# First expert group with seven half products, a ring of five x tiles, and shorter latencies in the planner's table

## The chip, the cores and the metric

The kernel runs on one core of one Trainium2 chip. The metric is the device time of one execution in microseconds (us); the smaller, the better. Five engines work side by side: PE (matrix products), DVE (VectorE), ACT (ScalarE), POOL (GpSimd) and SP, which here issues all DMA transfers.

## The reference

One transformer block, all in float32, with S = 2048 tokens and D = 512:

```python
xn = layernorm(x)
# A: sliding-window attention, 32 heads of 16, window of 256 keys
p = softmax(where(mask, q @ k.T / 4, -1e9));  a = (p @ v) @ wo
# B: 8 experts, F = 1376; top 8 of 8, so every expert counts for every token
gates = softmax(xn @ w_gate)
b = sum(gates[:, e] * (silu(xn @ w1[e]) @ w2[e]) for e in range(8))
out = x + a + b
```

## The kernel before

**Numbers.** Each float32 operand of a product is split into a high and a low half in float16. A product is then three matmuls: high by high, high by low, low by high. The helper `mm3` (lines 259 to 261) writes these three. Each matmul has a weight load (LDWEIGHTS) of its own.

**Tiling of the experts.** The hidden columns of the eight experts are cut into 17 groups of 128-column pairs: for each expert one group of two pairs and one of three, and after expert 3 a mixed group of three pairs from the seams between experts. Tokens are in four blocks of 512 (`tb`). A "double" is the work of `first_products` on two (pair, block) units; there are 70 doubles. Where a group has three pairs, the middle double of three takes the third pair for two token blocks at once.

**First products** (xn by w1) use Strassen's scheme in Winograd's form: seven half products in place of eight. The seven token-side operands ("x factors", numbered 0 to 6) of each block are made once, stored to the DRAM tiles `XS`, and read back for each double by `load_x_part`: 728 loads of 256 KB, all from SP (L710), into a ring of `XB` = 8 tiles `xs`. A load may start when the product that read the tile's old content has ended. A double whose two units have the same block takes seven tiles, a middle double fourteen.

**Second products** (h by w2) come in two forms. `second7` also uses seven half products, in steps of 256 columns on two halves of two PSUM banks, with five evictions by DVE per pair of 128-row stripes (`evict`, e1 to e5). `second` is the plain form: per stripe of 128 rows, for each 128-column piece of the pair, one `mm3` of 512 columns, and one eviction of 512 columns per stripe. Before the change the groups of three pairs of one expert (`part`) and those of two pairs (`seven`) take `second7`, but group 0 is left out of `seven`; group 0 and the mixed group take `second`. For `second7` DVE or POOL form four sums of the activations (`sum7`) and ACT with DVE or POOL split seven factors (`factor7`, tiles `hh` and `hl`, `HB` = 18 of each); w2 is split into four sets of "half weights" A to D (`prep2s`, with four sums by POOL) in place of the two pieces of `prep2`. The half weights lie in `W2B` = 16 slots.

**What sets the order.** The program of every engine is laid out by hand. A planner (`Order`) runs while the program is written: it keeps a clock for PE (`order.t`) and one each for ACT, DVE, POOL and SP, adds a fixed cost for each instruction, and appends an instruction when its inputs are ready by these clocks. A result counts as ready at the planned end plus `LATE` of the engine (for PE: plus `DRAIN`) plus `AGO` = 100 ns; a load on SP is booked with 450 ns for its issue, and then 2000 ns and 899 ns for its data, behind the loads booked before it (`landed`). Before PE's next piece `wait` looks whether its inputs are ready; if not, it puts other work first: steps of attention (`attend`) or second products (`drain_one`); only with none left does it let PE's clock run idle. On the chip each engine runs its list in order and waits on semaphores; the planner's times no longer matter then, only the order that came of them.

Of the kernel before, what the change touches and what calls it, by code (L numbers as in the profile page):

```python
# [18 lines left out]
P = 128  # L19
# [28 lines left out]
HB = 18  # L48
XB = 8
W2B = 16  # L50
# [8 lines left out]
DRAIN = 200  # L59
# [18 lines left out]
LATE = {"A": 100, "V": 80, "G": 80}  # L78
# [172 lines left out]
def tile_attn_moe(ctx: ExitStack, tc: tile.TileContext, x, wqkv, wo, _bx, wg, w1, w2, out):  # L251
# [103 lines left out]
    seven = {g for g, (e, pairs) in enumerate(groups) if len(pairs) == 2 and g}  # L355
# [119 lines left out]

    def prep2(g, i, j, r2, slot, act, dve):
        w = w2s[g, i, j]

        def high():
            w["t"] = moe.tile([P, 2, D], F16, tag=f"w2_{slot}", bufs=1, name=f"w2_{g}_{i}_{j}")  # L480
            nc.scalar.activation(out=w["t"][:, 0, :], in_=r2()[:, j, :], func=AF.Copy, scale=power[g][0][:, 1:2])

        def low():
            nc.vector.scalar_tensor_tensor(
                out=w["t"][:, 1, :], in0=r2()[:, j, :], scalar=power[g][0][:, 1:2], in1=w["t"][:, 0, :],
                op0=ALU.mult, op1=ALU.subtract,
            )

        w["done"] = dve(665, low, [act(615, high, [])])

    def prep2s(g, i, r2, slots, act, dve, gps):
# [3 lines left out]
        def part(src, kind, o, n, hilo):  # L495
            w = w2s[g, i, kind]

            def run():
                if "t" not in w:
                    w["t"] = moe.tile([P, 2, D], F16, tag=f"w2_{slots[kind][0]}", bufs=1, name=f"w2_{g}_{i}{kind}")  # L500
                sc = power[g][0][:, 1:2]
                hi, lo = (w["t"][:, p, o : o + n] for p in range(2))
                if hilo == 0:
                    nc.scalar.activation(out=hi, in_=src(), func=AF.Copy, scale=sc)
                else:
                    nc.vector.scalar_tensor_tensor(out=lo, in0=src(), scalar=sc, in1=hi, op0=ALU.mult, op1=ALU.subtract)
# [190 lines left out]
    x_issued = Event(0)  # L697

    def load_x_part(free, slack):
# [8 lines left out]
        def run():  # L708
            t = moe.tile([P, 2, 2, TB // 2], F16, tag="xs", bufs=XB, name=f"xs{m}_{b[0]}_{b[1]}")
# [456 lines left out]
    def weight_tasks():  # L1166
# [3 lines left out]
        slots2 += [((-2,), None)] * (W2B - 4 - len(slots2)) + [((-1,), {"gone": xn_free})] * 4  # L1170
        preps = {g: [] for g in range(NG)}
# [212 lines left out]
    with tc.tile_pool(name="ph0", bufs=1) as p0:  # L1384
# [183 lines left out]
        def layernorm(tb, slack):  # L1568
# [4 lines left out]
                    moe.tile([P, 2, 2, TB // 2], F16, tag="xs", bufs=XB, name=f"x{r}{c}").rearrange(  # L1573
                        "p r k t -> p r (k t)"
                    )
# [378 lines left out]
        for tb in range(4):  # L1954
# [20 lines left out]
            if tb == 3:  # L1975
                for n in range(XB):
                    had = (16 + n - XB) // 4
# [349 lines left out]
```

## Time and profile before

| | us |
|---|---|
| median of 3 runs (2070.85 to 2072.74) | 2072.7 |
| the profiled execution | 2072.15 |
| its span, first to last instruction | 2070.4 |
| PE busy in the span | 2034.6 (98%) |
| DVE busy | 1732.4 (84%) |
| ACT busy | 1356.9 (66%) |
| POOL busy | 997.1 (48%) |

The busy time of an engine is the time in which at least one of its instructions is in work. On PE a matmul of 256 columns is shown with 0.27 us though the next starts 0.11 us later, since they are pipelined; the rate is read from the starts. The idle time of an engine before an instruction is put down to what ended it (the releaser).

### The profile page before, as it was taken

Reading aid. Unit: us, or ns where it says so; the run is one execution under the profiler, and the core shown is the slowest. Engines: PE = TensorE matmul, PEld = TensorE weight load, DVE = VectorE, ACT = ScalarE, POOL = GpSimd, SP = SyncE. Lnnn points to the kernel's source line nnn. Section 1 sums busy time; section 2 is a strip of 40 time slices with the busy share of each in tenths; the row PEclk is TensorE's granted clock in tenths of the full one; section 3 lists DMA queues with packets and bytes.
Section 4 is the critical chain, followed back from the end, with each engine's and each line's share of the span. In section 5 each row is a group of like instructions: output and inputs, shape, how many; then the busy total and the mean of one; then the engine's idle time right before and its main releaser. Section 6 shows DMA issues by size and latency. Waiting matters only on the chain.

```text
span 2070.4 us, 52097 instructions
## 1 busy us (share of the span) xinstructions
PE 2034.6 (98%) x20036; PEld 1687.9 (82%) x20036; DVE 1732.4 (84%) x3594; ACT 1356.9 (66%) x2438; POOL 997.1 (48%) x1113
## 2 busy tenths in 40 slices
PE   7999999999999999999999999999999999999999
PEld 4657788888888888888876688888888888888887
DVE  7547887998889988998866889889988998889967
ACT  5656767666666766775656667676767667766753
POOL 5533545555355544563433445445544455356632
PEclk9999999999999999999999999999999999999999
DMA  6875557455654665476776545664656456645642
GB/s 222 260 239 190 171 186 210 130 156 166 204 148 116 220 203 155 110 214 191 210 214 218 166 137 160 196 171 119 201 178 187 112 177 174 217 126 142 173 151 81
DMA packets 343418, 362.16 MB, mean 175 GB/s; under 512 B 132192, under 2 KB 211040, under 8 KB 343168
## 3 DMA queue, kind: packets, MB, share of 16 engines
q1 hardware_dynamic: 343168, 358.82, 57.8%
q8 instruction: 157, 2.57, 0.5%
q14 instruction: 93, 0.76, 0.1%
HBM read 324.55 MB, written 33.88 MB: 173 GB/s over the span
## 4 chain that ended last, share of the span: by engine, by line
PE 86%; DVE 7%; DMA 3%; ACT 2%; issue 1%; SPq 1%; POOL 0%; DVEq 0%; POOLq 0%; ACTq 0%
PE acc L259 11%; PE acc L260 11%; PE acc L261 11%; PE zx L259 6%; PE zx L261 6%; PE zx L260 6%; PE zy L259 5%; PE zy L261 5%; PE zy L260 5%; PE pv L2142 4%; PE qk L1753 4%; PE st L2110 3%; PE sc L2042 3%; PE vg L1816 2%; DMA r<-in_B_w_dram 2%; DVE x L123 1%
## 5 line engine op out<-in xcount | busy, mean ns | idle before, releaser
L123 DVE SCALAR_TENSOR_TENSOR x<-acc,gsc,x 128x512 f32<-128x512 f32 x616 | 392.2, 640 | 110.9 <-PE acc L261 105.9
L259 PE MATMUL zx<-xs,w 128*128 128x256 f16 x1376 | 375.5, 273 | 2.4 <-DMA xs<-XS 2.3
L261 PE MATMUL zx<-xs,w 128*128 128x256 f16 x1376 | 375.1, 273 | 0.0
L260 PE MATMUL zx<-xs,w 128*128 128x256 f16 x1376 | 375.0, 272 | 0.0
L2096 ACT ACTIVATE pf<-st,esc 128x512 f32<-128x512 f32 (+2 forms) x384 | 245.9, 657 | 105.4 <-PE st L2110 104.1
L259 PE MATMUL zy<-xs,w 128*128 128x256 f16 x1032 | 281.6, 273 | 6.8 <-DMA xs<-XS 3.2
L261 PE MATMUL zy<-xs,w 128*128 128x256 f16 x1032 | 281.3, 273 | 0.0
L260 PE MATMUL zy<-xs,w 128*128 128x256 f16 x1032 | 281.2, 272 | 0.0
L260 PEld LDWEIGHTS <-w 128*128 128x128 f16 x2408 | 235.4, 98 | 49.2 <-issue 11.4
L259 PEld LDWEIGHTS <-w 128*128 128x128 f16 x2408 | 234.9, 98 | 45.1 <-issue 5.2
L123 DVE CUSTOM_DVE_ANT_0 sc<-sc,mask 128x320 f32<-128x320 f32 (+4 forms) x512 | 235.2, 481 | 39.7 <-PE sc L2042 38.2
L261 PEld LDWEIGHTS <-hl 128*128 128x128 f16 x2288 | 222.9, 97 | 44.6 <-POOL hl L123 0.7
L261 PEld LDWEIGHTS <-w 128*128 128x128 f16 x2408 | 234.8, 98 | 28.1
L260 PEld LDWEIGHTS <-hh 128*128 128x128 f16 x2288 | 223.7, 98 | 41.8 <-issue 6.8
L978 ACT ACTIVATE hh<-s 128x512 f16<-128x512 f32 x304 | 186.4, 625 | 107.5 <-DVE s L123 46.7
L259 PEld LDWEIGHTS <-hh 128*128 128x128 f16 x2288 | 223.2, 98 | 37.7 <-issue 5.5
L123 POOL TENSOR_SCALAR_AFFINE_SELECT pf<-pf 128x512 f32<-128x512 f32 (+1 forms) x256 | 155.1, 615 | 184.4 <-ACT pf L2096 94.9
L123 POOL TENSOR_TENSOR hl<-s,hh 128x512 f16<-128x512 f32 x126 | 147.5, 1177 | 85.3 <-ACT hh L978 34.2
L123 POOL TENSOR_TENSOR sums<-r 128x256 f32<-128x256 f32 x162 | 122.8, 758 | 131.7 <-DMA r<-in_B_w_dram 46.8
L123 POOL TENSOR_TENSOR sums<-r,sums 128x256 f32<-128x256 f32 x119 | 90.1, 757 | 157.4 <-DVE hl L123 47.0
L123 POOL TENSOR_TENSOR hl<-zb,hh 128x512 f16<-128x512 f32 x88 | 102.6, 1166 | 118.9 <-ACT hh L978 80.1
L123 DVE TENSOR_TENSOR hl<-s,hh 128x512 f16<-128x512 f32 x178 | 142.1, 806 | 14.1 <-ACT hh L978 13.7
(206 smaller groups left out, 5513.6 us busy)
## 6 DMA issues: line engine op xcount, KB each, us to landing
xs<-XS SPq DMA_DIRECT2D x728, 256.0 KB, 3.2
r<-in_B_w_dram SPq DMA_DIRECT2D x172, 256.0 KB, 3.8
r<-in_B_w_dram SPq DMA_DIRECT2D x80, 512.0 KB, 4.8
OS<-os SPq DMA_DIRECT2D x64, 128.0 KB, 2.1
q<-QS SPq DMA_DIRECT2D x192, 32.0 KB, 2.3
VS<-vt SPq DMA_DIRECT2D x16, 256.0 KB, 2.9
ot<-OS SPq DMA_DIRECT2D x128, 32.0 KB, 2.0
lt<-RS SPq DMA_DIRECT2D x128, 32.0 KB, 2.7
```

What stands on the lines that cost most here:

```text
L123: one = getattr(self.engine, name)(*args, **kw)
L259: nc.tensor.matmul(ps, lhsT=lh, rhs=rh, start=first, stop=False, **kw)
L260: nc.tensor.matmul(ps, lhsT=lh, rhs=rl, start=False, stop=False, **kw)
L261: nc.tensor.matmul(ps, lhsT=ll, rhs=rh, start=False, stop=last, **kw)
L978: nc.scalar.activation(out=h["hi"], in_=src(), func=AF.Copy)
L1753: nc.tensor.matmul(ps, lhsT=a[w][c // 2][:, k, cs], rhs=b[k // 2][:, k % 2, :], start=n == 0 and k == 0, stop=n == 2 and k == KC - 1,)
L1816: nc.tensor.matmul(ps[:, : VW // 2], lhsT=a[k // 2][:, k % 2, ts], rhs=b[2][:, k, ws], start=n == 0 and k == 0, stop=n == 2 and k == KC - 1,)
L2042: nc.tensor.matmul(ps[:, :n], lhsT=s.q[:KR, j * P : (j + 1) * P], rhs=s.k[:KR, cs : cs + n], start=True, stop=True)
L2096: nc.scalar.activation(out=w["pf"][:, j0 * P :], in_=ps[:, j0 * P :], func=AF.Exp, scale=esc)
L2110: nc.tensor.matmul(ps[:, j * P : (j + 1) * P].rearrange("p (b c) -> p b c", c=64), lhsT=s.k[:QR, kc : kc + P], rhs=of_head(s.q[:QR, qc : q ...
L2142: nc.tensor.matmul(ps[VC * j : VC * j + VC, a * P : (a + 1) * P], lhsT=s.v[:, kb, a * VC : a * VC + VC], rhs=w["pf"][:, j * P : (j + 1) * ...
```

## The change

- `seven` takes group 0 too: its second products go through `second7`, its activations through `silu7`, `sum7` and `factor7`, its w2 through `prep2s`.
- The ring of x tiles has `XR` = 5 tiles (tags xs0 to xs4) in place of 8. The three other tiles of the old ring, xs5 to xs7, become slots for half weights (`place2`) once the last products of phase 0 have read them. `W2B` falls to 15, so there are 18 slots. In phase 0 the layernorm still uses all eight.
- `HB` rises from 18 to 19.
- The planner's latencies: `DRAIN` 200 to 110, `LATE` for ACT 100 to 10, for DVE 80 to 40, for POOL 80 to 10.

```diff
-HB = 18
+HB = 19
 XB = 8
-W2B = 16
+XR = 5
+W2B = 15
...
-DRAIN = 200
+DRAIN = 110
...
-LATE = {"A": 100, "V": 80, "G": 80}
+LATE = {"A": 10, "V": 40, "G": 10}
...
-    seven = {g for g, (e, pairs) in enumerate(groups) if len(pairs) == 2 and g}
+    seven = {g for g, (e, pairs) in enumerate(groups) if len(pairs) == 2}
...
+    def place2(slot, name):
+
+        if slot < W2B:
+            return moe.tile([P, 2, D], F16, tag=f"w2_{slot}", bufs=1, name=name)
+        t = moe.tile([P, 2, 2, TB // 2], F16, tag=f"xs{XR + slot - W2B}", bufs=1, name=name)
+        return t.rearrange("p r k t -> p r (k t)")
...
-            t = moe.tile([P, 2, 2, TB // 2], F16, tag="xs", bufs=XB, name=f"xs{m}_{b[0]}_{b[1]}")
+            t = moe.tile([P, 2, 2, TB // 2], F16, tag=f"xs{next(x_turn) % XR}", bufs=1, name=f"xs{m}_{b[0]}_{b[1]}")
...
+        slots2 += [((-1,), {"gone": qk_gone[1, 1]})] * (XB - XR)
...
-                for n in range(XB):
-                    had = (16 + n - XB) // 4
+                for n in range(XR):
+                    had = (XB + n) // 4
```

By the two orders the change takes 192 matmuls of 512 columns from PE and adds 336 of 256 columns, and 144 weight loads. DVE gets 16 evictions of 256 columns and 8 of 512 more; ACT 16 instructions more; POOL 50 more, since the planner now gives it more of the sums and low halves; SP has as many DMAs as before, 1994.

On PE, the first second products of group 0, ahead of the change (names: `acc` the PSUM tile, `w2_0_0_0` the first piece of the first pair's weights, `hh` and `hl` the high and low half of the activations, `zy` and `xs` a first product):

```order
L259 LDWEIGHTS hh_2256
L259 MATMUL acc_2310<-w2_0_0_0_1612,hh_2256 128x512
L260 LDWEIGHTS hh_2256
L260 MATMUL acc_2310<-w2_0_0_0_1612,hh_2256 128x512
L261 LDWEIGHTS hl_2257
L261 MATMUL acc_2310<-w2_0_0_0_1612,hl_2257 128x512
L259 LDWEIGHTS w1_0_0_1595
L259 MATMUL zy_2318<-xs3_0_1_2198,w1_0_0_1595 128x256
```

And in the same place with the change (`w2_0_0D` is half weight set D):

```order
L260 LDWEIGHTS hh_2104
L260 MATMUL acc_2273<-w2_0_0D_1612,hh_2104 128x256
L261 LDWEIGHTS hh_2104
L261 MATMUL acc_2273<-w2_0_0D_1612,hh_2104 128x256
L262 LDWEIGHTS hl_2105
L262 MATMUL acc_2273<-w2_0_0D_1612,hl_2105 128x256
L260 LDWEIGHTS hh_2104
L260 MATMUL acc_2273<-w2_0_0D_1612,hh_2104 128x256
```

One `mm3` of 512 columns has become two of 256, one for each pair, and the first of them stands within the first product of the next double; ahead of the change it stood behind that double's third product.

On SP, the start of the first middle double (group 1, third pair, blocks 0 and 1; `xs4_1_0` is x factor 4 for group 1, block 0; `r1` raw weights; `OS` a store of attention), ahead of the change:

```order
L710 DMA xs0_1_0_3191<-XS0_63 128x1024
L710 DMA xs0_1_1_3247<-XS1_64 128x1024
L2160 DMA OS_60<-os_3263 128x256
L710 DMA xs1_1_0_3299<-XS0_63 128x1024
L710 DMA xs1_1_1_3327<-XS1_64 128x1024
L370 DMA r1_2_1_3333<-in_B_w1_dram 128x4x256
L710 DMA xs4_1_0_3381<-XS0_63 128x1024
L710 DMA xs4_1_1_3408<-XS1_64 128x1024
```

With the change:

```order
L719 DMA xs0_1_0_3462<-XS0_63 128x1024
L719 DMA xs0_1_1_3491<-XS1_64 128x1024
L719 DMA xs1_1_0_3544<-XS0_63 128x1024
L719 DMA xs1_1_1_3580<-XS1_64 128x1024
L719 DMA xs4_1_0_3605<-XS0_63 128x1024
L719 DMA xs4_1_1_3640<-XS1_64 128x1024
L719 DMA xs3_1_0_3646<-XS0_63 128x1024
L387 DMA r2_1_1_3659<-in_B_w2_dram 128x512 x2
```

The first seven loads of this double now follow each other with nothing between, and each waits for the tile of the load five ahead of it, not eight.

On DVE, around the first eviction of group 0, ahead of the change (`x0` takes the sum, `ISA sc` is the maximum of attention's scores):

```order
L123 SCALAR_TENSOR_TENSOR t_2437<-t_2428,za_2303 128x512
L123 SCALAR_TENSOR_TENSOR x0_124<-acc_2310,gsc_1871,x0_124 128x512
L123 TENSOR_REDUCE m_2451<-mp_1514 128x2
L123 ISA sc_2461,mt_2309<-sc_2461,mask_106 128x64
L123 ISA mt_2309 128x1
L123 SCALAR_TENSOR_TENSOR x0_124<-acc_2433,gsc_1871,x0_124 128x512
```

With the change (`s7` a sum of activations):

```order
L124 SCALAR_TENSOR_TENSOR x0_124<-acc_2273,gsc_1877,x0_124 128x256
L124 SCALAR_TENSOR_TENSOR zb_2154<-t_2281,zb_2154 128x2x256
L124 TENSOR_TENSOR s7_2318<-za_2064,zb_2154 128x512
L124 TENSOR_TENSOR s7_2331<-s7_2318,za_2064 128x512
L124 TENSOR_TENSOR hl_2329<-s7_2318,hh_2328 128x512
L124 SCALAR_TENSOR_TENSOR za_2348<-zy_2292,s1_2299 128x2x256
L124 TENSOR_SCALAR mh_2345<-mT_2343 16x128
L124 SCALAR_TENSOR_TENSOR x0_124<-acc_2311,gsc_1877,x0_124 128x512
```

Between two evictions DVE now also makes sums and a low half, which group 0 didn't need there before.

## Rows read from the trace of the kernel before

**Rows 1.** The page: busy time, share of the span and instructions of each engine, and the granted TensorE clock in 40 slices.

```profile
span 2070.4 us, 52097 instructions
PE 2034.6 (98%) x20036; PEld 1687.9 (82%) x20036; DVE 1732.4 (84%) x3594; ACT 1356.9 (66%) x2438; POOL 997.1 (48%) x1113
...
PEclk9999999999999999999999999999999999999999
```

**Rows 2.** What PE waited for: line, releaser, us in total, times, longest.

```profile
PE tp L1636 <- DVE xn L123: 7.0, 2, 6.6
PE acc L259 <- DVE x L123: 4.7, 8, 1.3
PE zy L259 <- DMA xs<-XS: 3.2, 5, 1.1
PE zx L259 <- DMA xs<-XS: 2.3, 3, 1.0
...
PE zy L259 <- DVE za L123: 2.0, 4, 0.8
...
PE sc L2042 <- DVE mt L123: 1.1, 3, 0.5
PE sc L2042 <- ACT pf L2096: 1.1, 2, 0.7
PE zy L259 <- ACT zb L1065: 0.9, 3, 0.4
PE st L2110 <- DVE mt L123: 0.8, 2, 0.4
...
PE acc L261 <- POOL hl L123: 0.2, 1, 0.2
```

**Rows 3.** The timeline of PE in group 0's second products, first and last of twelve matmuls of 512 columns in a row (start, duration).

```profile
175.80 0.38 PE L259 MATMUL acc<-w,hh 128*128 128x512 f16 x1
...
178.17 0.38 PE L261 MATMUL acc<-w,hl 128*128 128x512 f16 x1
```

**Rows 4.** The timeline in group 1: first and last of nine second-product matmuls of 256 columns in a row, twice, the DVE eviction behind the first nine, and an ACT instruction with the DVE instruction that waits for its result.

```profile
300.54 0.27 PE L259 MATMUL acc<-w_0A,hh 128*128 128x256 f16 x1
...
301.42 0.27 PE L261 MATMUL acc<-w_2A,hl 128*128 128x256 f16 x1
...
301.73 0.75 DVE L123 SCALAR_TENSOR_TENSOR x<-acc,gsc,x 128x512 f32<-128x512 f32 x1 [0.91 <-PE acc L261]
...
302.41 0.27 PE L259 MATMUL acc<-w_0D,hh 128*128 128x256 f16 x1
...
302.61 0.72 ACT L428 ACTIVATE w<-sums,sc 128x512 f16<-128x512 f32 x1
...
303.28 0.27 PE L261 MATMUL acc<-w_2D,hl 128*128 128x256 f16 x1
...
303.37 0.75 DVE L123 SCALAR_TENSOR_TENSOR w<-sums,sc,w 128x512 f16<-128x512 f32 x1
```

**Rows 5.** Groups of instructions by line and form: count, busy us, mean ns of one, idle before.

```profile
L260 PEld LDWEIGHTS <-hh 128*128 128x128 f16 x2288 | 223.7, 98 | 41.8 <-issue 6.8
...
L123 DVE SCALAR_TENSOR_TENSOR x<-acc,gsc,x 128x512 f32<-128x512 f32 x376 | 279.6, 744 | 86.8 <-PE acc L261 83.3 <-PE sc L2042 0.9 <-PE mb L1235 0.2
L123 DVE TENSOR_TENSOR hl<-s,hh 128x512 f16<-128x512 f32 x178 | 142.1, 806 | 14.1 <-ACT hh L978 13.7
L123 DVE SCALAR_TENSOR_TENSOR x<-acc,gsc,x 128x256 f32<-128x256 f32 x240 | 114.3, 476 | 24.0 <-PE acc L261 22.6 <-PE mb L1235 0.5
L978 ACT ACTIVATE hh<-s 128x512 f16<-128x512 f32 x304 | 186.4, 625 | 107.5 <-DVE s L123 46.7 <-PE acc L260 33.2 <-POOL s L123 26.6
L123 POOL TENSOR_TENSOR hl<-s,hh 128x512 f16<-128x512 f32 x126 | 147.5, 1177 | 85.3 <-ACT hh L978 34.2 <-DVE hl L123 14.7 <-DVE s L123 9.3
```

**Rows 6.** Busy time of PE, PEld, DVE, ACT and POOL (and instructions) in stretches of 50 us, then granted clock, DMA share and GB/s.

```profile
150.00:200.00 50.00, 49.34 (x406) 35.27 (x404) 34.63 (x91) 30.89 (x55) 16.00 (x19) 1.00 0.64 207
200.00:250.00 50.00, 50.00 (x444) 35.20 (x443) 39.03 (x86) 35.85 (x64) 25.27 (x32) 1.00 0.51 145
...
600.00:650.00 50.00, 50.00 (x484) 44.36 (x483) 48.30 (x86) 31.44 (x55) 26.16 (x26) 1.00 0.42 124
...
1150.00:1200.00 50.00, 47.56 (x388) 32.72 (x387) 43.71 (x90) 30.99 (x54) 24.55 (x29) 1.00 0.55 162
```

**Rows 7.** All instructions on the tiles `xs`: the loads (count, issue ns min/median/max), and the time from issue to landing.

```profile
L710 SPq DMA_DIRECT2D xs<-XS x728: 319/326/1814, 122.8 to 2022.3; - x182
...
DMA to landing us min/median/max: 2.6/3.2/7.7
```

**Rows 8.** The timeline of SP ahead of two stretches in which PE waited for x tiles (start, time to the end of the last, count).

```profile
317.54 0.39 SPq L2160 DMA_DIRECT2D OS<-os  x1
317.98 3.31 SPq L710 DMA_DIRECT2D xs<-XS  x7
...
472.39 9.88 SPq L710 DMA_DIRECT2D xs<-XS  x13
```

**Rows 9.** Busy time in stretches of 3 us where PE waited for x tiles, as in rows 6.

```profile
321.00:324.00 3.00, 2.04 (x20) 1.68 (x20) 2.36 (x8) 0.78 (x2) 0.00 (x0) 1.00 0.87 266
...
478.00:481.00 3.00, 2.24 (x22) 1.85 (x20) 2.01 (x5) 1.37 (x3) 0.00 (x0) 1.00 1.04 377
```

More of the change, by code (lines that the diff above doesn't have):

```diff
@@ L479, in high @@
         def high():
-            w["t"] = moe.tile([P, 2, D], F16, tag=f"w2_{slot}", bufs=1, name=f"w2_{g}_{i}_{j}")
+            w["t"] = place2(slot, f"w2_{g}_{i}_{j}")
             nc.scalar.activation(out=w["t"][:, 0, :], in_=r2()[:, j, :], func=AF.Copy, scale=power[g][0][:, 1:2])
@@ L499, in run @@
                 if "t" not in w:
-                    w["t"] = moe.tile([P, 2, D], F16, tag=f"w2_{slots[kind][0]}", bufs=1, name=f"w2_{g}_{i}{kind}")
+                    w["t"] = place2(slots[kind][0], f"w2_{g}_{i}{kind}")
                 sc = power[g][0][:, 1:2]
@@ L697, in tile_attn_moe @@
     x_issued = Event(0)
+    x_turn = iter(range(10**9))
     def load_x_part(free, slack):
@@ L1572, in layernorm @@
                 [
-                    moe.tile([P, 2, 2, TB // 2], F16, tag="xs", bufs=XB, name=f"x{r}{c}").rearrange(
-                        "p r k t -> p r (k t)"
-                    )
+                    moe.tile(
+                        [P, 2, 2, TB // 2], F16, tag=f"xs{(4 * tb + 2 * r + c) % XB}", bufs=1, name=f"x{r}{c}"
+                    ).rearrange("p r k t -> p r (k t)")
                     for c in range(2)
```

## The prediction

> **What bounds the kernel now.** First the page: PE is busy 98% of the span at the full clock, DVE 84%, ACT 66%, POOL 48% [rows 1]. Busy time on PE counts pipelined matmuls, so I looked at the starts next: in second products the starts of twelve matmuls of 512 columns lie (178.17 - 175.80) / 11 = 0.2155 us apart [rows 3], those of nine of 256 columns (301.42 - 300.54) / 8 = 0.11 us [rows 4]. PE runs without gaps in most stretches of 50 us (50.00 of 50 at 200 and at 600 us [rows 6]). So the end is set by PE's work, and by PE's waits: the span less its busy time is 2070.4 - 2034.6 = 35.8 us. Of these 7.0 are the first layernorm, mostly before the first matmul; 10.6 us in 22 waits are for DVE and ACT (4.7 + 2.0 + 1.1 + 1.1 + 0.9 + 0.8), and 5.5 us in 8 waits for x tiles [rows 2]; the rest is scattered, or lies behind the last matmul. What the change is worth is then: PE's work saved, plus what it does to these waits. All sums are made against the profiled execution, 2072.15 us: the span and 1.75 us around it. It lies 0.55 us below the median, inside the three runs. A change of 0.2% (4.1 us) is about what a measurement of this kernel can tell from none.
>
> **Part 1: the second products of group 0.** Taken away: 192 x 0.2155 = 41.4 us. Added: 336 matmuls of 256 columns at 0.11 us; with the eight steps from 302.41 to 303.28 it is (0.88 + 0.87) / 16 = 0.1094 [rows 4], so 336 x 0.1094 = 36.7 us. Net **-4.7 us**, on the path as it stands, since PE is the bound. (At a flat 0.11 it would be -4.4.) The 144 added weight loads take 98 ns each [rows 5]; they are issued beside the running matmul, and nothing of them shows in a pitch of 109 ns, so they cost nothing. That cover is thin, 11 ns for each; without it they would cost 144 x 0.098 = 14.1 us (rival 5).
>
> The Trainium skill says otherwise: "TensorE: Matmul & The Clock Gate", section "Back-to-back issue gap", gives a sustained spacing of about 131 ns for 512 columns and 81 ns for 128 in a stream of weight loads and matmuls, and calls 216 ns the isolated gap. By that the removed matmuls would be worth 192 x 0.131 = 25 us and the added ones, estimated midway at 0.098, 33 us: a loss of 8 us. Here the sustained spacing is 0.2155 us in a stream with one weight load for each matmul [rows 3], so the trace disagrees with 131 ns, and the sum goes by the trace.
>
> **Part 2: what group 0 adds to DVE, ACT and POOL.** DVE: 16 x 0.476 + 8 x 0.744 = 13.6 us of evictions [rows 5], some 2.4 us more for splitting half weights, and the part of 28 low halves and 16 sums that the order gives to it in group 0, 10 and 6, about 16 x 0.7 = 11 us: 27 us in the about 80 us of group 0 (150 to 230). DVE had 34.6 + 0.6 x 39.0 = 58 us of 80 there [rows 6], so it comes to about 85. These durations overlap at their ends by some tenth, so in truth it is near full, not over. ACT (12 high halves x 0.625, and a few splits: +10 us) and POOL (+50 instructions x about 1.2 us over the whole kernel, 48% to 51%) have room. Does a full DVE hold PE up? At 600 us DVE is busy 48.30 of 50 and PE 50.00, at 1150 us DVE 43.7 and PE loses 2.4 us [rows 6]. So between 0 and 2.4 us per 50 us; over group 0 and the first half of group 1, about 127 us of PE's work, 0 to +6 us. I take 0: the row at 600 us is the nearer one, being ordinary group work, while 1150 us is the end of the mixed group; and over the whole kernel DVE loses 14 other sums and low halves (of 0.8 us [rows 5]) to POOL.
>
> **Part 3: five x tiles.** An x tile's time, from the last matmul on its old content to the first on its new, has to hold PE's signal to SP (about 0.2 us, as from PE to DVE: 301.42 + 0.11 to 301.73 [rows 4]), the issue, and the landing, 2.6 us at least, 3.2 in the median, 7.7 at most, counted from the issue's start [rows 7]: 3.4 us typically. Counted in the orders with the pitches above, this time was never under 6.7 us before and under 8 us for 28 of 720 loads; with five tiles it goes down to 3.6 us, is under 6 us for 78 of 723, and under 8 us for 191, nearly all of the tight ones in the middle doubles, which eat two tiles in each product. SP's list stays as long, and a load that waits there holds the DMAs behind it: attention's `q`, `k` and raw weights, mostly needed tens of us later. The upper end: before, 143 loads had less than 12 us, and 8 waits came (one in 18), 0.69 us each. Now 396 loads have less than 12 us: 22 waits, 15 us, +10 us; should those under 6 us wait one time in four, it is 37 waits, +20 us. The lower end: the waits of before stand behind bursts, seven loads at 318 us and thirteen at 472 us [rows 8], which SP issued at once after being held up, so that the DMA engines were full (share 0.87 to 1.04) while PE starved [rows 9]. Five tiles cannot make such bursts, so a few of the 5.5 us may go: -3. I take **+0.7 us**, one more wait, because the tightest time, 3.6 us, still holds the typical 3.4: the planner books each load at 450 + 2899 ns and lets other work go ahead of a product whose tile it doesn't expect.
>
> **Part 4: the planner's latencies.** They only move instructions. By the rows the new ones are close: the PE to DVE step above is 0.20 us, the table now gives 110 + 100 = 210 ns, before 300. ACT's high half takes 0.625 us and the next engine starts about 0.04 us later (302.61 + 0.72 to 303.37 [rows 4]), 665 ns in all; the planner's cost 525 + `LATE` + 100 is now 635, before 725. The DVE eviction: 744 + 40 = 784 against 805, before 845. POOL's low half: 1177 + 40 = 1217 against 1240, before 1310. So a step loses 40 to 90 ns of margin, and of the 22 waits for DVE and ACT each may grow by a step or two, 22 x 0.18 = +4 us; against that, engine lists that follow true times have fewer instructions in the wrong turn, at best half of the 10.6 us: -5. I take 0.
>
> **Part 5: more tiles.** A nineteenth factor tile and 18 half-weight slots for 16: ACT waited 33.2 us for a factor tile's release (`hh` <- PE acc [rows 5]), but PE waited 0.2 us for a factor [rows 2], and for no half weight. Between 0 and -1; I take 0.
>
> **Sum.** 2072.15 - 4.7 + 0 + 0.7 + 0 + 0 = **2068.1 us**.
>
> **The rivals.**
> 1. The forecast: the saving arrives, the waits stay within 4 us of what they were: 2064 to 2072.
> 2. The ring starves PE. In the middle doubles tiles arrive late because a load's landing is over 4 us when raw weights or attention's pieces share the DMA engines. For it: the tight times, landings up to 7.7 us [rows 7], PE's losses of a third of 3 us when DMA is full [rows 9]. Against it: the planner's bookings, and no more bytes. Price +10 to +20, middle +15: 2072.15 - 4.7 + 15 = 2082.4 us, slower. It decides from the point where the loads with under 6 us wait more often than one time in ten (8 more waits, 5.5 us).
> 3. DVE becomes the bound in groups 0 and 1, or the thinner margins lengthen the short waits: +4 to +6 in place of 0: 2072.15 - 4.7 + 5.3 = 2072.7 us, no change. For it the row at 1150 us, against it the row at 600 us [rows 6].
> 4. Truer latencies and more tiles take away half of the waits for DVE and ACT: 2072.15 - 4.7 - 5.3 = 2062.2 us. For it: the new table is within 35 ns of the rows, the old one 60 to 100 ns off; against it: less margin for each.
> 5. The change doesn't do what it says on PE: the weight loads come out from under the matmuls of 256 columns, as the thin cover of 11 ns would allow. 2072.15 - 4.7 + 14.1 = 2081.5 us. The trace speaks against it: 240 matmuls of each of these forms run at this pitch already. This is the direction in which the Trainium skill's rule in "TensorE: Matmul & The Clock Gate", section "Back-to-back issue gap", points.
>
> **How the numbers follow.** Rival 1 has 0.43, of which 0.30 below 2068.6 (0.2% under the median) and 0.13 above; its middle is close to that line, but a saving of work is certain and its cost isn't, so I lean to the lower side. Rival 2: 0.22. Rival 3: 0.20, 0.17 within 0.2% and 0.03 above. Rival 4: 0.13. Rival 5: 0.02. Faster 0.30 + 0.13 = 0.43; same 0.13 + 0.17 = 0.30; slower 0.22 + 0.03 + 0.02 = 0.27. The range goes from 2059 (rival 4 with a few us more) to 2083, which holds the larger half of rival 2; about 0.07 is left out below and 0.12 above. The likeliest case's own range is 2064 to 2072.
>
> **What would show it.** PE: the 192 matmuls `acc` of 128x512 gone and 336 more of 128x256 at 0.109 us. The waits of PE for `xs`: about 6 us in 9 (mine), 15 to 25 in over 20, in middle doubles (rival 2). The stretches 150 to 300 us: PE at 49 to 50 of 50 (mine), under 48 (rival 3). The sum of PE's waits for DVE and ACT: 7 to 15 us (mine), under 6 (rival 4), over 15 (rival 3). What would make the prediction wrong altogether is a new order with one long hold somewhere, several us on a gate row or a raw weight, which no row of before can show.

## The result, and the profile after

| | before | after |
|---|---|---|
| median, us | 2072.7 (6 runs) | 2086.3 (6 runs, 2084.3 to 2094.4) |
| the profiled execution | 2072.15 | 2087.07 |
| its span | 2070.4 | 2085.3 |

The ratio of after to before is 1.0071, with a 95% interval of 1.0056 to 1.0086: slower by 13.6 us, where 4.6 us less were forecast. The time is 3 us above the forecast's range.

The page after, the rows that answer to [rows 1]:

```profile
span 2085.3 us, 52410 instructions
PE 2034.3 (98%) x20180; PEld 1702.2 (82%) x20180; DVE 1746.3 (84%) x3608; ACT 1364.9 (65%) x2454; POOL 1055.5 (51%) x1163
```

PE has less work, and its busy time is the same to 0.3 us: part of it is spent on something else. Its idle time rose from 35.8 to 51.0 us. What PE waited for after (line, releaser, us in total, times, longest), against [rows 2]:

```profile
PE tp L1646 <- DVE xn L124: 8.7, 2, 6.3
PE zy L260 <- DMA xs<-XS: 7.8, 10, 2.0
PE zx L260 <- DMA xs<-XS: 6.8, 8, 2.2
PE acc L260 <- DVE x L124: 3.5, 9, 0.8
PE sc L2052 <- DMA RS<-lt: 2.6, 2, 1.3
PE zx L260 <- ACT s L1074: 2.3, 2, 1.8
...
PE zy L260 <- DMA q<-QS: 1.8, 1, 1.8
PE sc L2052 <- DVE mt L124: 1.6, 6, 0.5
...
PE mT L2059 <- ACT hh L987: 1.4, 1, 1.4
```

The waits for x tiles went from 5.5 us in 8 to 14.6 us in 18: +9.1 us, the largest single change. Second, the stretches in which group 0's second products run and end (PE, PEld, DVE, ACT and POOL busy, granted clock, DMA share, GB/s; 150 to 300 us, then stretches of 10 us):

```profile
150.00:300.00 150.00, 143.76 (x1437) 122.04 (x1436) 131.55 (x285) 105.38 (x188) 77.79 (x87) 0.98 0.59 179
200.00:210.00 10.00, 10.00 (x97) 8.87 (x96) 9.70 (x22) 6.89 (x11) 4.44 (x5) 1.00 0.58 183
210.00:220.00 10.00, 10.00 (x97) 8.87 (x95) 10.00 (x23) 6.71 (x12) 7.50 (x9) 1.00 0.27 80
220.00:230.00 10.00, 10.00 (x98) 8.91 (x96) 10.00 (x23) 6.96 (x13) 6.00 (x7) 1.00 0.53 155
250.00:260.00 10.00, 9.18 (x93) 7.92 (x90) 9.80 (x26) 8.57 (x16) 6.03 (x9) 1.00 0.74 233
260.00:270.00 10.00, 7.61 (x63) 5.60 (x66) 7.49 (x15) 6.14 (x11) 5.78 (x7) 0.66 0.64 179
```

The same stretch before, and ten of its microseconds:

```profile
150.00:300.00 150.00, 149.20 (x1346) 111.43 (x1343) 118.58 (x269) 102.12 (x182) 66.41 (x77) 1.00 0.59 184
240.00:250.00 10.00, 10.00 (x83) 7.38 (x81) 10.00 (x23) 7.85 (x14) 4.27 (x6) 1.00 0.52 148
```

Before, PE was busy for 149.20 of these 150 us and DVE for 118.58. Now DVE has no idle time at all for 20 us, PE loses nothing in that time, and pays between 250 and 290 us, most of it between 250 and 270. The timeline there, DVE, POOL and ACT (start, duration, idle before and releaser), then PE:

```profile
259.45 0.49 DVE L124 CUSTOM_DVE_ANT_0 sc<-sc,mask 128x320 f32<-128x320 f32 x1
259.86 0.53 DVE L124 CUSTOM_DVE_ANT_0 sc<-sc,mask 128x320 f32<-128x320 f32 x1
260.31 0.14 DVE L124 DVE_READ_ACCUMULATOR2_ANT mt<- 128x1 f32 x1
260.83 1.15 POOL L124 TENSOR_TENSOR hl<-zb,hh 128x512 f16<-128x512 f32 x1
262.01 0.60 ACT L1074 ACTIVATE zb<-zy 128x512 f32<-128x512 f32 x1 [1.52 <-POOL hl L124]
```

```profile
258.91 0.27 PE L262 MATMUL acc<-w_1A,hl 128*128 128x256 f16 x1
260.60 0.27 PE L2059 MATMUL mT<-ident,mt 128*16 128x128 f32 x1 [1.42 <-ACT hh L987]
262.66 0.37 PE L260 MATMUL zy<-xs,w 128*128 128x256 f16 x1 [1.79 <-DMA q<-QS]
262.82 0.42 PE L261 MATMUL zy<-xs,w 128*128 128x256 f16 x1
...
267.73 0.42 PE L260 MATMUL zx<-xs,w 128*128 128x256 f16 x1
...
268.24 0.27 PE L260 MATMUL zx<-xs,w 128*128 128x256 f16 x1
268.35 0.27 PE L261 MATMUL zx<-xs,w 128*128 128x256 f16 x1
```

The transposition `mT` starts 0.15 us after DVE has put out the last maximum `mt`. DVE works through its list without a pause there; it is simply behind. The next first product needs its bank, which ACT empties as `zb`; ACT had to wait for POOL to finish with the old `zb`. (The releaser shown for 262.66, a DMA of `q`, was named by its time; ACT's end at 262.61 is what fits, and in the run with eight tiles below the same wait of 2.87 us is named `zb`.) Then comes a cost of another kind: from 262.82 to 267.73 the matmuls start (267.73 - 262.82) / 23 = 0.2135 us apart, not 0.109. The granted clock of these matmuls is the lower level, 1.2 GHz, and PE had done one instruction between 259.2 and 262.66 us. From 262.66 to 268.24 there are 27 steps; they took 5.58 us in place of 27 x 0.109 = 2.95, so this costs 2.6 us, and it counts as busy time. The Trainium skill, "TensorE: Matmul & The Clock Gate", section "Wait — 56ns, not 53.3ns?", gives N / 1.2 GHz as the spacing at the lower clock; worked out from it, 256 columns take an estimated 213 ns. The trace agrees.

**Where the 14.9 us between the two profiled executions lie**: -4.7 of work; +9.1 for x tiles; between 150 and 300 us 6.24 - 0.80 = 5.4 us more idle, of which 0.9 are x tiles counted already, so +4.5; +2.6 for the clock. That is 11.5. The other 3.4 us are not traced to a cause: 1.6 us are idle time elsewhere, the balance of longer and shorter waits (2.6 us for `RS` are new), and 1.8 us are PE's busy time, which fell by only 0.3 us where -4.7 and +2.6 make -2.1.

**How an x tile comes late.** One wait in full. PE needs a tile at 450.6 us and gets it at 451.46. Its load on SP, and what stands ahead of it there:

```profile
437.18 1.03 SPq L2199 DMA_DIRECT2D lt<-OS  x2
438.31 0.36 SPq L221 DMA_DIRECT2D k<-KS  x1
438.72 1.84 SPq L221 DMA_DIRECT2D q<-QS  x2
...
445.11 1.84 SPq L2216 DMA_DIRECT2D ot<-OS  x4
447.04 0.37 SPq L2210 DMA_DIRECT2D lt<-RS  x1
447.45 0.42 SPq L2216 DMA_DIRECT2D ot<-OS  x1
447.92 0.42 SPq L2210 DMA_DIRECT2D lt<-RS  x1
448.39 0.41 SPq L719 DMA_DIRECT2D xs<-XS  x1
```

```profile
437.69 0.27 PE L262 MATMUL zx<-xs,w 128*128 128x256 f16 x1
...
451.46 0.28 PE L260 MATMUL zy<-xs,w 128*128 128x256 f16 x1 [0.83 <-DMA xs<-XS]
```

The matmul at 437.69 is the last reader of the tile's old content, so the tile was free at 437.80. The load was issued at 448.39, 10.6 us later, because SP first issued attention's loads, one every (447.04 - 445.11) / 4 = 0.48 us. It landed 3.0 us after its issue, an ordinary landing [rows 7]. SP wasn't waiting for PE at all: it was working through its list.

I did this for all loads: from the start of the tile's last reading matmul + 0.109 us to the load's issue. After, 143 of 723 loads were issued over 2 us late, and 21 of the 25 waits (those of over 60 ns from start to start) belong to them. Before, 176 of 720 loads were as late. So SP is no worse than it was; with eight tiles such a load had the time. What SP did in the meantime can be added up for the 143: of 719 us between free and issue (counted for each load) it was issuing DMAs for 585 us, 1294 of them, and only 54 us are pauses of over 0.15 us. So it is the number of issues ahead of the load, and not one DMA that waits there.

### The profile page after: what moved, and what is told of

It reads as the page before. It is cut to its first block, busy times and chain, and to the rows that moved or that the text cites. A ratio compares the mean times of both kernels' runs of the same rounds, so it can differ in the third digit from the quotient of the medians.

```text
span 2085.3 us, 52410 instructions
## 1 busy us (share of the span) xinstructions
PE 2034.3 (98%) x20180; PEld 1702.2 (82%) x20180; DVE 1746.3 (84%) x3608; ACT 1364.9 (65%) x2454; POOL 1055.5 (51%) x1163
## 4 chain that ended last, share of the span: by engine, by line
PE 81%; DVE 6%; DMA 4%; POOL 2%; ACT 2%; issue 2%; SPq 2%; POOLq 0%; DVEq 0%; ACTq 0%
PE acc L260 11%; PE acc L262 11%; PE acc L261 11%; PE zx L260 6%; PE zx L262 6%; PE zx L261 6%; PE zy L260 5%; PE zy L262 4%; PE zy L261 4%; PE pv L2152 4%; PE qk L1763 4%; DMA xs<-XS 3%; PE st L2120 3%; PE sc L2052 3%; PE vg L1826 2%
## 5 line engine op out<-in xcount | busy, mean ns | idle before, releaser
L124 DVE SCALAR_TENSOR_TENSOR x<-acc,gsc,x 128x512 f32<-128x512 f32 (+1 forms) x640 | 404.8, 637 | 95.9 <-PE acc L262 90.3
L987 ACT ACTIVATE hh<-s 128x512 f16<-128x512 f32 x320 | 194.7, 624 | 135.4 <-POOL s L124 54.3
L261 PEld LDWEIGHTS <-hh 128*128 128x128 f16 x2336 | 228.4, 98 | 39.2 <-issue 6.0
L262 PEld LDWEIGHTS <-hl 128*128 128x128 f16 x2336 | 227.7, 97 | 38.6 <-POOL hl L124 0.9
L260 PEld LDWEIGHTS <-hh 128*128 128x128 f16 x2336 | 228.0, 98 | 34.3 <-issue 4.0
L124 POOL TENSOR_TENSOR hl<-s,hh 128x512 f16<-128x512 f32 x157 | 181.3, 1164 | 75.5 <-ACT hh L987 28.6
L969 ACT ACTIVATE t<-zb,th 128x512 f32<-128x512 f32 x160 | 110.4, 690 | 52.3 <-DVE zb L124 49.6
```

Of the source, the lines that this page charges most:

```text
L124: one = getattr(self.engine, name)(*args, **kw)
L260: nc.tensor.matmul(ps, lhsT=lh, rhs=rh, start=first, stop=False, **kw)
L261: nc.tensor.matmul(ps, lhsT=lh, rhs=rl, start=False, stop=False, **kw)
L262: nc.tensor.matmul(ps, lhsT=ll, rhs=rh, start=False, stop=last, **kw)
L969: nc.scalar.activation(out=box["t"], in_=z(), func=AF.Tanh, scale=factors[g][1])
L987: nc.scalar.activation(out=h["hi"], in_=src(), func=AF.Copy)
```

## The experiments

In the table, "x tiles" is PE's waits for them, us and times; "idle" is 150 us less PE's busy time between 150 and 300 us.

| kernel | us | ratio | x tiles | idle |
|---|---|---|---|---|
| before | 2072.7 | | 5.5, 8 | 0.8 |
| null change of before | 2075.8 | 1.0009 to 1.0027 | 3.2, 6 | 1.5 |
| latencies alone | 2079.7 | 1.0022 to 1.0047 | 3.1, 5 | 2.1 |
| ring alone | 2091.5 | 1.0072 to 1.0099 | 17.7, 18 | 3.9 |
| group 0 alone | 2072.5 | 0.9993 to 1.0011 | 3.3, 3 | 6.8 |
| after | 2086.3 | 1.0056 to 1.0086 | 14.6, 18 | 6.2 |
| null change of after | 2086.3 | 1.0056 to 1.0082 | 9.2, 17 | 5.2 |
| after, group 0 undone | 2087.8 | 1.0065 to 1.0090 | 10.3, 19 | 3.0 |
| after, latencies undone | 2093.3 | 1.0090 to 1.0117 | 8.5, 14 | 8.4 |
| after, ring of 8 | 2084.1 | 1.0045 to 1.0070 | 3.0, 4 | 6.5 |
| after, ring of 8, again | 2097.8 | 1.0108 to 1.0136 | 2.7, 3 | 6.6 |
| after, ring of 7 | 2075.4 | 1.0008 to 1.0025 | 3.3, 5 | 6.9 |
| before, merged DMAs | 2067.6 | 0.9970 to 0.9987 | 0, 0 | 0.6 |
| ring alone, merged DMAs | 2063.5 | 0.9947 to 0.9973 | 3.3, 5 | 1.2 |
| after, merged DMAs | 2066.1 | 0.9962 to 0.9982 | 2.1, 4 | 3.9 |

**First: undo one part, or do one alone.** After with eight tiles (W2B 16, HB 18):

```diff
-XR = 5
-W2B = 15
-HB = 19
+XR = 8
+W2B = 16
+HB = 18
```

> Undoes the ring and the extra tiles: the changed kernel with a ring of 8 x tiles, 16 half-weight slots, 18 factor tiles; group 0 in seven half products and the new latencies stay. In the changed kernel PE waited 14.6 us in 18 waits for x tiles (before: 5.5 in 8), and had one hold near 260 us (1.6 + 1.9 us of waiting, then 26 matmuls at half the clock, about 2.7 us). Theory R (the ring starves PE): waits for x tiles fall to about 5 us in 8, the time to 2086.3 - 9.5 = 2077 us, and to 2071 if the hold near 260 us goes with the new order. Theory L (the shorter latencies put PE ahead of its tiles): waits for x tiles stay over 10 us, time 2083 to 2087. Theory O (any new order scatters some us of waits): 2075 to 2083 with the waits in other places.

After with the old latencies:

```diff
-DRAIN = 110
-LATE = {"A": 10, "V": 40, "G": 10}
+DRAIN = 200
+LATE = {"A": 100, "V": 80, "G": 80}
```

> Undoes the latencies alone: the changed kernel with DRAIN 200 and LATE 100/80/80; five x tiles, group 0 in seven half products and 19 factor tiles stay. Theory R: waits for x tiles stay at 12 to 18 us in 15 to 22, time 2083 to 2088. Theory L: waits for x tiles fall under 8 us, short waits for DVE and ACT too, time about 2072. Theory O: within 5 us of 2086 with no pattern; the hold near 260 us may go (-6).

After with group 0 in the plain form again:

```diff
-    seven = {g for g, (e, pairs) in enumerate(groups) if len(pairs) == 2}
+    seven = {g for g, (e, pairs) in enumerate(groups) if len(pairs) == 2 and g}
```

> Undoes group 0 alone: the changed kernel with group 0's second products in the plain form again; five x tiles and the new latencies stay. Adds 4.7 us of matmuls by the measured pitches. Theory R: waits for x tiles stay at 12 to 18 us; the hold near 260 us, which stands behind a full DVE, goes (-6.2): 2086.3 + 4.7 - 6.2 = 2085 us. If group 0's load on DVE were the main cause, waits for x tiles would fall as well and the time be 2074 or less. Theory L: as theory R here, 2085.

The ring alone is that edit, the old latencies and HB 18 together.

> The ring alone: the kernel before with five x tiles, the three others as half-weight slots (18), 18 factor tiles; old latencies, group 0 plain. Theory R: waits for x tiles rise from 5.5 to 12 to 18 us, time 2072.7 + 7 to 12 = 2080 to 2085 us. Theory L: waits for x tiles at 5 to 8 us, time 2071 to 2075. Theory O: 2070 to 2078.

The ring alone costs 19 us, and undoing it in the changed kernel takes x tiles' waits back to 3.0 us, as theory R has it. But the time with eight tiles hardly fell: other waits had come. PE's waits in that run begin so:

```profile
PE zy L260 <- ACT zb L1074: 9.2, 11, 2.9
PE tp L1646 <- DVE xn L124: 8.8, 2, 6.4
PE acc L260 <- DVE x L124: 6.0, 11, 1.2
```

Undoing the latencies made it slower, though the waits for x tiles fell to 8.5 us, so theory L, that the shorter margins starve the ring, does not explain the time. Theory R misses the time, theory O gains weight: how much does any new order cost?

**Null changes, and the other two parts alone.** A null change makes nothing costlier and only lets the planner come to another order, a new draw. In the table of before and of after, DRAIN moved by 2 ns (200 to 202, 110 to 112):

> The kernel before with one number of the planner's table moved by 2 ns: DRAIN 202 in place of 200. Nothing is costlier, but the order written for PE differs from the old one in about a quarter of its rows. Theory O (the order of before is a lucky draw among many, and every other draw has more waits, whatever made it): 2077 to 2088 us, with 8 us or more of added waits of PE for DVE, ACT or x tiles in places where before has none. Theory R (five x tiles and group 0's full DVE are what costs): 2069 to 2075 us, waits for x tiles about 5 us.

> The changed kernel with DRAIN 112 in place of 110, a null change likewise. Theory O: anywhere from 2070 to 2092, with other waits than the changed kernel. Theory R: waits for x tiles again 12 to 18 us, time 2083 to 2089, and the hold near 260 us, which comes of group 0's work on DVE, again of 3 to 6 us.

Before with group 0 in `seven`, and before with the new latencies:

> Group 0 alone: the kernel before with group 0 in seven half products; ring of 8, old latencies, 18 factor tiles and 16 slots. Theory R: waits for x tiles about 5 us; 2072.4 - 4.7 + 0 to 6 (a hold near 260 us, as in the changed kernel) = 2068 to 2074. Theory O: 2072 to 2084, with new short waits spread over the whole span, far behind group 0.

> The latencies alone: the kernel before with DRAIN 110 and LATE 10/40/10. Theory L (shorter margins make PE wait for results): short waits of PE for DVE and ACT rise by 5 to 15 us, all over the span, time 2078 to 2088, and more than in the null change of the kernel before. Theory O: as the null change within 5 us. Theory R: 2069 to 2075.

A null change costs before 3.7 us (0.18%) and after nothing. It keeps each one's pattern: few waits for x tiles with eight tiles, many with five. But the size of these waits is itself a draw: the seven kernels with five tiles and attention's DMAs as they are on SP have 8.5 to 17.7 us of them, and the null change of after has 9.2 in place of 14.6 at the same median. So +9.1 us is what they cost in one order. Theory O in its strong form (every order 8 us worse than that of before) is out. Group 0 alone brings nothing, 2072.5, though PE's work fell as counted; its row for 150 to 300 us:

```profile
150.00:300.00 150.00, 143.25 (x1459) 123.01 (x1458) 132.51 (x291) 106.95 (x190) 72.49 (x81) 1.00 0.61 185
```

DVE is busy 132.5 us there, before 118.6, and PE idles 6.8 us, before 0.8. The latencies alone cost 7 us (0.34%), twice the null change. PE's waits for DVE and ACT rose by 11 us in that run and by 5 in the null change, as theory L has it.

**Then: SP's list, or the landing?** The 16 loads `lt` and `ot` of each output step become two, the nine of `q` and `k` of each pair of heads two; 448 of SP's 1992 DMAs go, with (nearly) all bytes kept, but attention's values come from the wrong rows (the trace counts 1992, two fewer than stated ahead of the prediction):

```diff
-        for r in range(3):
-            rows = slice(2 * p * DH, 2 * (p + 1) * DH)
-            move(kf[2 * r * DH : 2 * (r + 1) * DH, : s.nk], KS[r // 2, rows, s.k0 : s.k0 + s.nk], 2 * DH, 2560)
...
+        move(kf[:KR, : s.nk], KS[0, o : o + KR, s.k0 : s.k0 + s.nk], KR, 2560)
...
-            got = [order.move(1, partial(spread, h), [t], 9000 + 1500 * h, LOADED, DH, 2048) for h in range(8)]
+            got = [order.move(1, spread, [t], 9000, LOADED, P, 2048)]
```

> The ring alone (as in the run of the ring alone, 2091.5 us, PE's waits for x tiles 17.7 us in 18), with attention's small DMAs merged: the sixteen loads of each output step (lt and ot) become two of the same bytes and the same piece size, the nine loads of q and k of each pair of heads become two; 448 of SP's 1994 DMAs go. It takes these values from the wrong rows of DRAM, so it leaves out the right attention values; all matmuls and bytes stay. Theory Q (a tile is free in time, but its load stands behind other DMAs on SP's list, each 0.47 us): loads issued over 2 us after their tile came free fall from 145 to under 80, waits for x tiles to 8 us or less, time to 2076 to 2082. Theory B (the landing is slow because the DMA engines are full): same bytes, so waits for x tiles stay over 14 us, time 2087 to 2092.

> Control: the kernel before with the same merged DMAs (wrong rows for attention's values, as above). Theory Q: with eight tiles the late issues are mostly covered; waits for x tiles fall from 5.5 to 2 to 5 us, time 2066 to 2073. Theory B: as before, 2070 to 2075.

> The changed kernel with the same merged DMAs (wrong rows for attention's values). Theory Q: waits for x tiles fall from 14.6 us to 6 or less, the time to 2086.3 - 9 = 2077 or less; the hold near 260 us, which is of DVE, stays (3 to 6 us). Theory B: waits for x tiles over 11 us, time 2083 to 2088.

For the x tiles this decides between the two. The hardware queue's row (packets, MB, share of the 16 DMA engines), the x loads (count, size, median us from issue to landing) and PE's waits for x tiles, of the ring alone:

```profile
q1 hardware_dynamic: 343168, 358.82, 58.0%
...
xs<-XS SPq DMA_DIRECT2D x728, 256.0 KB, 3.2
...
PE zy L260 <- DMA xs<-XS: 10.3, 8, 2.2
PE zx L260 <- DMA xs<-XS: 7.4, 10, 2.1
```

and of the same with merged DMAs:

```profile
q1 hardware_dynamic: 336000, 358.79, 58.9%
...
xs<-XS SPq DMA_DIRECT2D x728, 256.0 KB, 3.0
...
PE zy L260 <- DMA xs<-XS: 2.2, 3, 1.1
...
PE zx L260 <- DMA xs<-XS: 1.1, 2, 1.0
```

The bytes and the DMA engines' share are the same and a load lands as fast as before, so full DMA engines (theory B) are not the cause. Loads issued over 2 us late fell from 145 to 48, and the time by 28.0 us, further than theory Q had it; in the changed kernel by 20.3 (late loads from 143 to 67), in the kernel before only by about 5. The x tiles' part of the 28.0 is 17.7 - 3.3 = 14.4 us. Another 7.0 us lie in PE's busy time, 2039.7 us in the ring alone and 2032.7 with merged DMAs, and the clock is part of it: in the ring alone it stood at the lower level for 6.9 us around a wait of 5.0 us for ACT at 723 us, and for 3.4 us behind a wait for an x tile (the matmul with its wait, then the busy times and the granted clock, 0.50, behind it):

```profile
170.34 0.28 PE L260 MATMUL zy<-xs,w 128*128 128x256 f16 x1 [2.15 <-DMA xs<-XS]
170.60:174.00 3.40, 3.40 (x19) 2.42 (x17) 0.69 (x1) 1.69 (x4) 0.82 (x1) 0.50 0.27 57
```

Past its start the merged kernel has one such stretch, of 3.4 us. The other 6.6 us are mostly shorter waits for ACT: 6.0 us for `zb` became 1.7, 4.1 for `pf` became 0.9. With a light list the ring of five shows no cost: 2063.5 against 2067.6, one order of each.

After with seven tiles:

```diff
-XR = 5
+XR = 7
```

> The changed kernel with seven x tiles in place of five (one tile left for half weights); group 0 in seven half products, new latencies, 19 factor tiles. Loads with under 8 us by the pitches: 73, against 191 with five and 19 with eight. Theory Q: waits for x tiles 4 to 8 us, near those of eight (3.0); time 2081 to 2086, since with eight it is still 2084. Theory B: the same waits, so this run sizes the ring and doesn't part the two.

The waits for x tiles are those of eight; the time, 2075.4, lay below what was expected.

**Does the order on SP's list do it, with every DMA kept?** The x loads' due time 8 us earlier:

```diff
-                load_x_part([ev], 8000)
+                load_x_part([ev], 0)
```

> The ring alone (five x tiles, old latencies, group 0 plain; 2091.5 us, waits of PE for x tiles 17.7 us, 145 loads issued over 2 us after their tile came free) with the x loads due 8 us earlier in the planner, so that they go ahead of attention's DMAs that are ready at the same time. No DMA is added or removed. Theory Q (order on SP's list): fewer late issues (under 110), waits for x tiles 8 to 13 us, time 2078 to 2086. If the number of DMAs on SP counts and not their order: 2088 to 2093, waits for x tiles over 15 us.

> The changed kernel with the x loads due 8 us earlier in the planner, nothing else. Theory Q: late issues fall from 143 to under 110, waits for x tiles from 14.6 to 6 to 10 us, time 2078 to 2083. Number and not order: 2084 to 2089.

> Group 0 alone on the kernel before (eight x tiles, old latencies; 2072.5 us) with the x loads due 8 us earlier. With eight tiles only 3 us of waits for x tiles are there to be had: 2069 to 2075, no change beyond the scatter of a new order (about 4 us, as the null change of the kernel before showed).

A second draw with eight tiles (W2B 15 and HB 19 kept):

> The changed kernel with eight x tiles, now with 19 factor tiles and 15 half-weight slots, where the first such run had 18 and 16 (2084.1 us; PE's waits for DVE and ACT large, for x tiles 3 us). If the shorter latencies cost steadily (theory L), it is again 2081 to 2087, with over 25 us of waits for DVE and ACT. If 2084 was a bad draw of the order (theory O): 2072 to 2080, as the run with seven tiles (2075.4).

With early x loads the three took 2092.4, 2098.7 and 2084.6 us (ratios 1.0074 to 1.0106, 1.0110 to 1.0142, 1.0041 to 1.0067). The last two lie outside everything expected; the first has the time that was expected if the number counts and not the order (2088 to 2093), with the waits for x tiles of theory Q. The waits for x tiles fell, from 17.7 to 10.9 us, from 14.6 to 12.9, and from 3.3 to none, but loads over 2 us late stayed 150 and 155 with five tiles, and other waits took the gain and more. So the due time is no cure. The second draw, 2097.8 us, is 13.7 us above the first, which has one factor tile less, one slot more and as few waits for x tiles; with seven tiles it is 2075.4. So between three kernels with group 0, the new latencies and few waits for x tiles lie 22 us, far more than the 4 us that I had expected of a draw, and a single kernel can't tell what the latencies cost. Whether all of it is the draw isn't shown: the slowest has 15 half-weight slots, fewer than any other kernel here.

**Last: SP's list relieved with every value kept, and DVE in group 0.** ACT issues `lt` and `ot` in place of SP:

```diff
-                nc.sync.dma_start(box["lt"][h * DH : (h + 1) * DH, :], src.partition_broadcast(DH))
+                nc.scalar.dma_start(box["lt"][h * DH : (h + 1) * DH, :], src.partition_broadcast(DH))
...
-            got = [order.move(1, partial(spread, h), [t], 9000 + 1500 * h, LOADED, DH, 2048) for h in range(8)]
+            got = [Later([order.task("A", 480, partial(spread, h), [t], 9000 + 1500 * h)], 2500) for h in range(8)]
```

> The changed kernel with the sixteen loads lt and ot of each output step issued by ACT, not SP: 256 DMAs leave SP's list, all bytes and values stay, and ACT gets 256 issues more. Theory Q: PE's waits for x tiles fall from 14.6 us to 6 to 10 us, late issues (over 2 us after the tile came free) from 143 to under 110; the time 2078 to 2084, unless ACT's issues hold back its own results (waits for ACT over 15 us: then 2084 to 2090). If the number of DMAs on SP's list is not the cause: waits for x tiles stay over 12 us.

2117.6 us (1.0198 to 1.0231): worse than either theory allowed, and a lesson of its own. ACT's timeline in that run:

```profile
703.44 0.71 ACT L512 ACTIVATE w_2B<-sums,sc 128x512 f16<-128x512 f32 x1
708.13 0.84 ACTq L2210 DMA_DIRECT2D lt<-RS  x2
709.02 0.47 ACT L2106 ACTIVATE pf<-st,esc 128x256 f32<-128x256 f32 x1 [4.87 <-DMA RS<-lt]
```

An `lt` load must wait until the store `RS` has landed. On ACT's list it holds all that stands behind it, here the `pf` of attention for 4.9 us. By the planner's clock the store had landed by then; on the chip it had not. Late loads fell to 116 of 723, yet the x tiles' waits stayed at 13.5 us. By the sign set beforehand (over 12 us) this speaks against the number of DMAs on SP as the cause. The trace shows why it doesn't settle it: between free and issue of the waited-for loads SP now issued 90 DMAs, in the changed kernel 197, but its pauses of over 0.15 us rose to 19 of 68 us, there 2 of 103. Another hold has taken the place of the old one; as it stands this is no way out.

Group 0 alone without its 28 low halves:

```diff
-            h["lo"] = moe.tile([P, 2, TB // 2], F16, tag="hl", bufs=HB, name="hl")
+            h["lo"] = moe.tile([P, 2, TB // 2], F16, tag="hl", bufs=HB, name="hl") if n >= 28 else h["hi"]
...
+        if n < 28:
+            h["low"] = h["high"]
+        elif early:
```

> Group 0 alone on the kernel before (2072.5 us) without the 28 low halves of group 0's activations: PE multiplies by the high half twice in their place, so group 0's second products lose their low part; PE's work is the same, DVE and POOL do 28 subtractions of 0.8 and 1.2 us less between 150 and 250 us. Theory D (DVE and POOL are behind there): the waits of PE for results between 150 and 300 us fall from 8.6 us to 4 or less, time 2066 to 2070. Theory E (the half products' evictions and banks make the waits): they stay at 7 us or more, time 2070 to 2075.

2081.3 us (1.0034 to 1.0058). DVE's busy time between 150 and 300 us fell from 132.5 to 126.0, PE's idle time there from 6.8 to 4.7, half way between the two expectations (from start to start, as above, the waits fell from 8.6 to 5.2 us). The total rose by waits elsewhere. That fits DVE's and POOL's load being part of it, but doesn't show it: 4.7 us lies inside the 3.9 to 8.4 us that the draws with group 0 in seven half products spread over.

## Why the prediction was wrong

- **What bounds the kernel**: right. PE sets the end, and every microsecond is one of its work, its waits or, new, its clock.
- **Part 1, -4.7 us**: right. The 192 matmuls went, the 336 came, 144 more weight loads (20180 against 20036) cost nothing to be seen; in group 0 alone PE's busy time is 2030.2 us against 2034.6, -4.4 us. Rival 5 is out. By the rule in the Trainium skill's "TensorE: Matmul & The Clock Gate", section "Back-to-back issue gap", PE's work would have risen; the trace doesn't bear that out.
- **Part 2, taken at 0 of 0 to +6**: a term mis-sized. The eleven kernels with group 0 in seven half products (without the one that has no low halves) idle 3.9 to 8.4 us between 150 and 300 us, 6.1 in the mean; the eight plain ones 0.6 to 3.9, 1.9 in the mean. So it costs some 4 us, and the clock's 2.6 us in the changed kernel on top, which no part had. The step that failed is the choice of the row at 600 us as the nearer one: at a DVE of 97% PE lost nothing there, and nothing at 100% from 210 to 230 us either. The loss comes later, at 250 to 290 us, where group 1 begins and PE waits for DVE's, POOL's and ACT's results. That it is the backlog of the full stretch is read from the two waits shown above; no run separates it, and before itself had a full DVE from 240 to 250 us at no loss. A full stretch has to be read together with the one behind it.
- **Part 3, taken at +0.7 of -3 to +20**: this step failed. It measured x waits of 14.6 us, +9.1, near the +10 that I gave as a bound: counting the loads with under 12 us gave 22 waits and 15 us, the trace has 18 and 14.6. I set the tightest time, 3.6 us, against signal, issue and landing, 3.4 us, as if SP were free when a tile comes free. I looked at what a waiting load holds up behind it, and not at what holds up the load: one load in five stands over 2 us behind other DMAs, most of them attention's. [rows 7] show the time from issue to landing, and nothing of the time from free to issue; the trace of before had it (176 late loads of 720), and I didn't take it out. For the same reason my point of decision, loads with under 6 us, was the wrong one: the 78 of them had 7 of the 25 waits, the 537 with 6 to 15 us had 18, the 108 with more none. The -3 for fewer bursts did not come, and the thirteen loads at 472 us [rows 8] were not all one burst: the last three were issued 1.5 to 2.0 us apart.
- **Part 4, 0 of -5 to +4**: not settled. By itself +7 us against +3.7 for a null change; with group 0 at eight tiles +11.6; with the ring -3.7, with both -7.0. With eight tiles they cost in both pairs, with five in neither; this and the spread between draws allow no size.
- **Part 5, 0**: not settled; it wasn't tried alone, and the two kernels with eight tiles, which differ only in these numbers (18 factor tiles and 16 slots, 19 and 15), lie 13.7 us apart.
- **The rivals**: rival 2 (the ring, +10 to +20) came about by the waits, +9.1, and by the ring alone, +19, but not by its mechanism of slow landings; rival 3 (results late in group 0 and behind it, +4 to +6) came with it. I had them as alternatives with a time each; together, from rows of after, -4.7 + 9.1 + 4.5 + 2.6 they explain 11.5 of 14.9 us. Neither excludes the other, and the range should have held both. Undoing the ring did not by itself bring the time back: 2084.1 and 2097.8 us with eight tiles, 2075.4 with seven.

No kernel that computes the reference was faster than before. Before, its null change, group 0 alone and seven tiles lie together at 2072 to 2076, and that is the best there is; the merged DMAs at 2063 to 2068 show what a shorter list on SP would be worth, with five tiles above all.

## What to carry to other kernels

Before a ring is made smaller, take from the trace when each slot came free and when its next load was issued, not only how long a load takes to land: a transfer queue that issues in order turns unrelated small DMAs into latency. What a full engine costs need not show in the full stretch; look for it also where its results are next needed. Parts that each cost something add up, so a range for a change of five parts has to hold two bad ones together; and where a planner writes the order, a null change measures how much of any difference is only another draw.

## What the runs showed that I had not expected

- The issue of a DMA occupied SP for about 0.48 us, for an `ot` piece of 32 KB as for an x load of 256 KB (seven in 3.31 us [rows 8]); 448 fewer of them brought 28.0 and 20.3 us with five tiles and 5 with eight, at the same bytes.
- After two gaps of 1.4 and 1.8 us with one short instruction between them, PE's next matmuls ran for 5.6 us at the lower clock level, 0.2135 us apart, which cost 2.6 us; the idle time doesn't show it, the granted clock of the stretch (0.66) does. In the ring alone it happened behind a single wait of 2.15 us, while the changed kernel's waits of 2.0 and 2.2 us for x tiles left the clock at full.
- A change of 2 ns in the planner's table moved before by 3.7 us and after by nothing; two kernels that differ by one factor tile and one half-weight slot lay 13.7 us apart.
- "Issuing engines are not separate DMA queues", a section of the Trainium skill's "DMA: Bandwidth & Descriptors", says that starting DMAs from several engines saves only the time of the issue, usually small beside the DMA. Here that time is the cost, 16 x 0.48 = 7.7 us for one output step, against 3.0 us from issue to landing of the load behind it; and moving it to ACT made 2117.6 us of 2086.3, since an issue that has to wait holds the engine's other work.
